# Opening set-up spread over ScalarE and VectorE, a second PSUM pool for one of the last sums, and a new table of priorities

## Chip, cores and metric

The kernel runs on 1 core of one Trainium2 chip. The metric is the device time of one execution in microseconds (us); the time before is the median of 3 runs, 860.9 us (860.76 to 861.0).

## The reference

Three stages follow one another: attention with a bucket mask, a gated feed-forward layer with an RMS norm, and a second feed-forward layer with an ELU.

```python
# q, k, v: (2, 8, 768, 64); proj: (64, 6)
q_bucket = sum over 6 bits of ((q @ proj) > 0) * 2**bit      # k_bucket likewise
scores = where(q_bucket[:, None] == k_bucket[None, :], q @ k.T / 8, -1e9)
attn = softmax(scores);  x = attn @ v         # x: (1536, 512), heads side by side
xn = x / sqrt(mean(x*x) + 1e-6) * rms_g
y  = (silu(xn @ w_gate) * (xn @ w_val)) @ w_out      # 512 -> 1536 -> 512
h  = y @ w_in                                        # 512 -> 2048
out = where(h > 0, h, exp(min(h, 0)) - 1) @ w_out2   # 2048 -> 512
```

## The kernel before

**Arithmetic.** TensorE works in fp32r; each fp32 operand is split into a rounded part (hi) and a remainder (lo), and products run in several passes.

**Attention.** The 16 heads are taken as 8 pairs (index j). The rows of a pair's q and k arrive in the tile raw by four DMAs (q and k of each of two heads a). twice (L326) copies each of the four into a tile rd, side by side with itself; prep_T (L337) transposes rd on TensorE in two halves (ps_t), ScalarE makes hi (L353), VectorE makes lo (L358), and GpSimd moves some rows across (L365, L368). prep_bits (L382) multiplies by the projection tile pj and VectorE writes the sign bits into one of two tiles bitt (L400). prep_count (L407) multiplies bitt by wsel to get the bucket match, which goes in as extra rows of the operands (L425, L427). Only then can score (L456) run: matmuls ps_s (L474), the row maximum nm on VectorE (L481), exp on ScalarE (L491), transposes of the weights ps_p (L519) with hi and lo (L527, L531), and the products with v (L566).

**The opening.** Before the first scores, ident and pj are made or cleared on GpSimd (setup, L1075), wsel is cleared there (L1100), and so are the two bitt tiles, with one row set to ones (setup_bits, L1102): a row that no bit is written to, so that the match carries a constant. VectorE writes a table of the numbers -1 and +1 for all bucket numbers (wtmp, setup_w), counts bits in ctmp (setup_count, L1089) and puts the parts of proj into pj (setup_pj, L1110). Small DMAs on the SP queue carry wtmp and ctmp into wsel. Dummy matmuls ps_w (L1143) keep TensorE at work from the moment ident exists.

**The feed-forward layers.** Weights arrive as 64-bit words, and ScalarE and VectorE turn them into fp32 (wf, L808 to L831), then into hi and lo (L852, L856). hidden makes ps_h (L905), reduce1 ps_y (L990), and reduce2 ps_o (L1044), which VectorE adds to the sums oa (L1056) before each block of 128 tokens is stored. ps_o uses the PSUM tag bank2 (2 buffers of two banks each); the tag bank has 4 buffers of one bank. The last block's columns are done in two cuts of 256.

**Order.** Nothing is issued as the code is written. Plan collects tasks with engine, assumed duration, reads and writes; Plan.order() lists them by earliest start and then by priority. The priorities of the attention tasks are a position (the unit number, 6 per pair, 48 in all) plus an entry of the table OFF; w0 and w0s in it place the first group of weights. Every engine then runs its own list in that order, so one changed assumption or entry can change the order of the whole attention stage.

```python
plan.add("DVE", 6.5, setup_count, [], [("h3", "ctmp")], -30)
plan.add("Pool", 3.1, setup_bits, [], ["bitt"], -29)
```

Of the kernel before, what the change touches and what calls it, by code (L numbers as in the profile page):

```python
# [12 lines left out]
AF = mybir.ActivationFunctionType  # L13
ALU = mybir.AluOpType
AX = mybir.AxisListType
# [7 lines left out]
PJP = -29.9  # L23
WARM = 16
POOL_COPY = 0.82
POOL_HALF = 0.57
POOL_CAST = 0.65
TURN = 0.13
BYPOOL = ([0, 1, 2, 3, 4], [0, 2, 3, 4], [0, 1, 2, 3, 4, 5], [2, 4], [2, 4], [2, 4], [2, 4], [0])
HOT = ('DVE', 'ACT', 'ACT', 'DVE')  # L30
BW = (384, 512)
OFF = {'S': [-0.384, -0.596, -1.82, 16.69, -0.785, -0.843, -0.281, -0.374], 'max': [107.091, 86.229, 74.287, 78.306, 4.65, 29.877, -1.002, 35.125], 'exp': [62.941, 112.551, 91.27, 19.546, 123.248, 62.234, 18.002, -5.545], 'T': [0.813, 0.913, 0.365, 0.876, 0.651, 1.113, 1.459, 0.993], 'hi': [19.733, -62.022, -7.959, -72.894, 51.659, 4.387, -74.284, -78.51], 'lo': [37.269, 76.285, 5.085, -95.768, -79.38, 8.342, -31.826, -0.586], 'V': [2.187, 1.975, 1.986, 1.909, 1.876, 2.208, 2.458, 2.096], 'my': [-17.276, -32.546, -64.73, -54.909, -121.029, -34.033, -7.347, -44.516], 'ld': [46.975, -7.846, 214.522, -35.192, 37.247, 221.876, -5.026, -66.279], 'pv': [56.573, -26.315, 46.952, -98.676, 75.721, 70.124, -94.292, -41.006], 'prep': [-0.879, -2.624, -3.589, -0.3, -0.223, -0.105, 0.276, -67.519], 'post': [5.051, 5.005, 2.459, 1.85, 3.722, 8.338, 2.173, 8.692], 'plo': [-134.549, 11.751, -83.073, -44.746, 0.084, -16.015, 72.021, -31.41], 'wc': -3.034, 'ld1': 96.489, 'norm0': -2.712, 'rush': 35.741, 'pstep': 0.316, 'qstep': 0.017, 'norm': 31.762, 'w0': 122.867, 'w0s': 1023313562453027.6}


class Plan:
# [143 lines left out]
def kernel(  # L179
# [14 lines left out]
    nc = tc.nc  # L194
    B, H, S, D = q.shape
    NB = proj.shape[1]
    NBK = 2 ** NB
# [4 lines left out]
    NC = S // 128  # L202
# [20 lines left out]
    def bank(name):  # L223
        return ps1.tile([128, 512], F32, tag="bank", name=name)

    def bank2(name):
        return ps2.tile([128, 2, 512], F32, tag="bank2", name=name)
# [11 lines left out]
    bitt = [const.tile([128, S], F32R, name=f"bitt{i}") for i in range(2)]  # L239
# [7 lines left out]
    plan = Plan(caps)  # L247

    def off(key, j):
        return OFF[key][j]  # L250

    def act(n, ptr=0):
        return n / 1200.0 + 0.05 + 0.093 * ptr

    def dve(n):
        return n / 960.0 + 0.069
# [10 lines left out]
    st = {}  # L267
# [57 lines left out]
        return (("slot", ("tq", "tk")[i], j, a), part)  # L325

    def twice(j, a, i, prio):
        def go():
            st["rd", j, a, i] = half([128, NC, 2, D], F32, "rd")
            nc.gpsimd.tensor_copy(  # L330
                out=st["rd", j, a, i], in_=st["raw", j][:, i, a].unsqueeze(2).to_broadcast([128, NC, 2, D])
            )

        plan.add("Pool", POOL_COPY, go, [(("slot", "raw", j), i, a)], [("h3", "rd", j, a, i)], prio)

    def prep_T(j, a, i, hf, prio):
        n = NC // 2  # L337
# [35 lines left out]
        if i == 0:  # L373
            plan.add("DVE", dve(HS), lo, [B_], top[:1], prio)
            plan.add("Pool", POOL_HALF, again, top[1:], [okey(j, a, i, ("dup", hf))], prio)
        else:
# [217 lines left out]
    def post(j, prio, step):  # L594
# [23 lines left out]

        plan.add("Pool", POOL_COPY, widen, [R_], [("h3", "rw", j)], prio)

# [137 lines left out]
    groups = []  # L758
# [17 lines left out]
    def weights(g, m, part, prio, gate):  # L776
# [19 lines left out]
        dma(load, 128 * cols * (8 if wide else 4), r=gate, w=[R_], prio=prio)  # L796
        prio += OFF["wc"]
        if wide:
# [232 lines left out]
    def reduce_cols(g, blk, t, tt, ds, prio):  # L1031
        li, f0, n, first, last = groups[g]
        wd = ds.stop - ds.start
        B_ = ("bank2", "o", g, tt, ds.start)
        A_ = ("slot", "oa", tt // 3)
        s = {}

        def pe(ft):
            if "ps" not in s:
                s["ps"] = bank2("ps_o")[:, 0, 0:wd]  # L1040
            wo = st["w", g]["wo"]
            h = st["h", g, blk, ft]
            for i, (wp, xp) in enumerate(PASS):
                nc.tensor.matmul(  # L1044
                    s["ps"], lhsT=h[:, xp, t * 128:(t + 1) * 128], rhs=wo[wp][:, ft, ds],
                    start=(ft == 0 and i == 0), stop=(ft == n - 1 and i == 2),
                )

        def copy():
            if ("oa", tt // 3) not in st:  # L1050
                st["oa", tt // 3] = slot([128, 3, DM], F32, "oa")
            nc.scalar.copy(out=st["oa", tt // 3][:, tt % 3], in_=s["ps"])

        def add():
# [14 lines left out]
        if first:
            plan.add("ACT", act(wd), copy, [B_], [(A_, tt % 3, 0)], prio)  # L1070
        else:
            plan.add("DVE", dve(wd), add, [B_], [(A_, tt % 3, ds.start)], prio)
        if last:
            dma(store, 128 * wd * 4, [(A_, tt % 3, ds.start)], [("out", tt, ds.start)], prio)
# [5 lines left out]
    def ones_of(t, i):  # L1080
        return t.rearrange("p (n t w) -> p n t w", t=2, w=2 ** i)[:, :, 1, :]
# [7 lines left out]
    def setup_count():  # L1089
        st["ctmp"] = half([1, 2, 2, NBK], F32, "ctmp")  # L1090
        c = st["ctmp"]
        nc.vector.memset(c[:, 1, 0], 0.0)
        for i in range(NB):
            t = ones_of(c[:, 1, 0], i)
            nc.vector.tensor_scalar(out=t, in0=t, scalar1=-1.0, scalar2=None, op0=ALU.add)
        nc.vector.tensor_copy(out=c[:, 1, 1], in_=c[:, 1, 0])
        nc.vector.tensor_scalar(out=c[:, 0], in0=c[:, 1], scalar1=1.0, scalar2=None, op0=ALU.add)

    def setup2():
        nc.gpsimd.memset(f(wsel), 0.0)  # L1100

    def setup_bits():  # L1102
        for t in bitt:
            nc.gpsimd.memset(f(t), 0.0)
            nc.gpsimd.memset(f(t[32:33]), 1.0)

    def setup3():
        nc.gpsimd.memset(ones, 1.0)
# [20 lines left out]
    plan.add("ACT", 0.02, lambda: nc.scalar.preload_act_table_set("natural_log_exp_and_others"), [], ["tab"], -40, tab="exp")  # L1129
    plan.add("Pool", 1.22, setup, [], ["ident", "pj0"], -30)  # L1130
    plan.add("DVE", 0.7, setup_w, [], [("h3", "wtmp")], -30)
    plan.add("DVE", 6.5, setup_count, [], [("h3", "ctmp")], -30)
    plan.add("Pool", 0.25, setup2, [], ["wsel0"], -29.5)
    plan.add("Pool", 3.1, setup_bits, [], ["bitt"], -29)
    plan.add("Pool", 0.2, setup3, [], ["ones"], -28)
    for a in range(2):
        dma(lambda a=a: ld_pj(a), 2000, [], [("pjf", a)], PJP)
# [24 lines left out]
    prep_v(0, -15)  # L1162
    load_qk(1, OFF["ld1"])

# [33 lines left out]
    for g in range(len(groups)):  # L1198
        li, f0, n, first, last = groups[g]
# [57 lines left out]
```

## Time and profile before

| what | value |
|---|---|
| median of 3 runs | 860.9 us |
| profiled execution, its own time | 861.95 us |
| its span, first to last instruction | 860.2 us |
| outside the span | 1.75 us |
| mean granted TensorE clock over the span | 0.995 |
| first scores on TensorE begin | 19.90 us |
| feed-forward work continuous on TensorE from | 302.56 us |
| last sum's matmuls begin | 855.60 us |

The span is what the rows below divide up. The profiled execution took 1.05 us longer than the median of the runs, 0.1%.

### The profile page before, as it was taken

To read this page: it belongs to the slowest core of one execution; us is meant where nothing else is said; L and a number is where in the kernel's file an instruction comes from. 1 tells how busy PE (TensorE), PEld (TensorE's weight loads), DVE (VectorE), ACT (ScalarE), POOL (GpSimd) and SP (SyncE) were. 2 spreads that over 40 slices of the span, in tenths; PEclk is the share of its full clock that TensorE was granted. 3 is DMA by queue.
4 is the path that set the end of the run, shared out by engine and by line. 5 is a ranking of instruction groups with operands and counts; after the bars stand their busy time and mean duration, and the time that the engine had idled before them with its cause. 6 is when DMAs were issued, how large, how long until landed. Compare 5 with 4: busy or idle time off the path is not lost.

```text
span 860.2 us, 12464 instructions
## 1 busy us (share of the span) xinstructions
PE 836.1 (97%) x4722; PEld 738.2 (86%) x4722; DVE 648.7 (75%) x1020; ACT 440.7 (51%) x831; POOL 279.2 (32%) x295
## 2 busy tenths in 40 slices
PE   7999999998999899999999999999999999999998
PEld 6899999887899799989889898887888888888786
DVE  8999899999999999443265555678856878677754
ACT  3889888898888655332222322245544333332321
POOL 8766576699745322110011110210201111111100
PEclk9999999999999999999999999999999999999999
DMA  5102012240002201211111312204221302001003
GB/s 165 39 19 64 12 38 75 60 146 35 19 2 75 74 1 38 85 31 44 49 50 50 98 50 99 74 1 146 74 74 37 110 25 74 25 25 50 1 12 135
DMA packets 25708, 49.05 MB, mean 57 GB/s; under 512 B 2480, under 2 KB 8880, under 8 KB 25648
## 3 DMA queue, kind: packets, MB, share of 16 engines
q1 hardware_dynamic: 25648, 48.25, 17.2%
q8 instruction: 37, 0.61, 0.3%
q14 instruction: 23, 0.19, 0.1%
HBM read 45.09 MB, written 3.15 MB: 56 GB/s over the span
## 4 chain that ended last, share of the span: by engine, by line
PE 80%; DVE 12%; ACT 4%; POOL 3%; issue 1%; POOLq 0%; DVEq 0%; ACTq 0%
PE ps_h L905 36%; PE ps_o L1044 14%; PE ps_y L990 11%; PE ps_s L474 5%; PE ps_v L566 5%; PE ps_p L519 5%; DVE pt L531 2%; PE ps_t L347 2%; DVE nm L481 2%; PE ps_b L395 1%; ACT p L491 1%; DVE wf L817 1%; DVE wf L824 1%; DVE wf L831 1%; ACT pt L527 1%
## 5 line engine op out<-in xcount | busy, mean ns | idle before, releaser
L856 POOL TENSOR_TENSOR wlo<-wf,whi 128x768 fp32r<-128x768 f32 (+1 forms) x54 | 87.4, 1618 | 444.8 <-ACT whi L852 430.5
L905 PE MATMUL ps_h<-xn,whi 128*128 128x512 f32 (+2 forms) x768 | 190.1, 336 | 2.9 <-DVE pt L531 1.1
L905 PEld LDWEIGHTS ps_h<-xn,whi 128*128 128x128 f32 x768 | 133.6, 189 | 15.6 <-DVE pt L531 1.4
L905 PE MATMUL ps_h<-xn,wlo 128*128 128x256 f32 (+2 forms) x384 | 128.9, 336 | 0.0
L1044 PE MATMUL ps_o<-whi,h 128*128 128x512 f32 (+1 forms) x388 | 118.9, 388 | 0.7 <-DVE oa L1056 0.6
L905 PE MATMUL ps_h<-y,whi 128*128 128x512 f32 x384 | 118.2, 389 | 0.0
L930 ACT ACTIVATE sg<-ps_h 128x512 f32<-128x512 f32 (+1 forms) x87 | 50.6, 583 | 112.6 <-PE ps_h L905 110.4
L852 ACT CAST whi<-wf 128x768 fp32r<-128x768 f32 (+1 forms) x54 | 39.6, 734 | 125.1 <-DVE wf L831 125.0
L566 PE MATMUL ps_v<-pt,vv 128*128 128x256 f32 x576 | 97.9, 296 | 2.2 <-DVE tk L358 1.0
L951 ACT CAST h<-hf 128x512 fp32r<-128x512 f32 (+1 forms) x87 | 51.7, 605 | 88.7 <-DVE hf L936 47.0
L481 DVE TENSOR_REDUCE nm<-ps_s 128x1 f32<-128x768 f32 x96 | 90.8, 946 | 3.1 <-PE ps_s L474 2.4
L990 PE MATMUL ps_y<-h,whi 128*128 128x512 f32 (+1 forms) x312 | 91.3, 373 | 1.3 <-DVE ya L1002 1.3
L491 ACT ACTIVATE p<-ps_s,nm 128x768 f32<-128x768 f32 x96 | 87.2, 909 | 8.3 <-DVE nm L481 7.6
L519 PE MATMUL ps_p<-ident,p 128*128 128x128 f32 x576 | 87.5, 278 | 3.4 <-DVE pt L531 2.6
L474 PE MATMUL ps_s<-tk,tq 128*128 128x384 f32 x384 | 88.2, 351 | 1.0 <-ACT p L491 0.9
L955 DVE TENSOR_TENSOR h<-hf,h 128x512 fp32r<-128x512 f32 (+1 forms) x87 | 69.5, 812 | 25.9 <-ACT h L951 25.1
L1044 PEld LDWEIGHTS ps_o<-whi,h 128*128 128x128 f32 x388 | 72.1, 188 | 16.7 <-DVE oa L1056 2.2
L905 PEld LDWEIGHTS ps_h<-y,whi 128*128 128x128 f32 x384 | 72.1, 188 | 15.0
L936 DVE TENSOR_TENSOR hf<-ps_h,sg 128x512 f32<-128x512 f32 (+1 forms) x39 | 25.2, 647 | 79.0 <-PE ps_h L905 79.0
L566 PEld LDWEIGHTS ps_v<-pt,vv 128*128 128x128 f32 x576 | 78.7, 189 | 5.4 <-DVE pt L531 1.9
L531 DVE TENSOR_TENSOR pt<-ps_p,pt 128x512 fp32r<-128x512 f32 x120 | 80.6, 681 | 3.6 <-ACT pt L527 2.2
L519 PEld LDWEIGHTS ps_p<-ident,p 128*128 128x128 f32 x576 | 67.3, 142 | 12.3 <-DVE pt L531 4.6
(109 smaller groups left out, 1521.3 us busy)
## 6 DMA issues: line engine op xcount, KB each, us to landing
wraw<-in_moe_w_out_dram SPq DMA_DIRECT2D x12, 768.0 KB, 5.1
wraw<-in_moe_w_in_dram SPq DMA_DIRECT2D x8, 768.0 KB, 4.7
wraw<-in_moe_w_out_dram SPq DMA_DIRECT2D x10, 512.0 KB, 4.0
raw<-in_q_dram SPq DMA_DIRECT2D x16, 192.0 KB, 3.1
raw<-in_k_dram SPq DMA_DIRECT2D x16, 192.0 KB, 3.5
vn<-in_v_dram SPq DMA_DIRECT2D x8, 384.0 KB, 3.2
wraw<-in_moe_w_gate_dram SPq DMA_DIRECT2D x4, 768.0 KB, 4.8
wraw<-in_moe_w_val_dram SPq DMA_DIRECT2D x4, 768.0 KB, 4.5
```

The costliest lines, as they stand in the source:

```text
L474: nc.tensor.matmul(st[B_][:, hf, 0:HS], lhsT=tq[:, x, c * 128:(c + 1) * 128], rhs=tk[:, x, hf * HS:(hf + 1) * HS], start=(x == 0), stop=(x ...
L481: nc.vector.tensor_reduce(out=st["nm", u, cc], in_=st[B_][:, :, 0:HS], axis=AX.XY, op=ALU.max, negate=True,)
L491: nc.scalar.activation(out=halves(st["p", u][:, cc]), in_=st.pop(B_)[:, :, 0:HS], func=AF.Exp, bias=st["nm", u, cc], scale=1.0, accum_out= ...
L519: nc.tensor.transpose(out=st[B_][:, o:o + 128], in_=p[:, cc, (2 * n + kt) * 128:(2 * n + kt + 1) * 128], identity=ident,)
L531: nc.vector.tensor_tensor(out=pt[:, 1], in0=st.pop(B_), in1=f(pt[:, 0]), op=ALU.subtract)
L566: nc.tensor.matmul(st[B_][:, 0:256], lhsT=st["vv", j][:, a, 2 * n + kt, :], rhs=pt[:, x, kt * 256:(kt + 1) * 256], start=(n == seq[0] and ...
L856: nc.gpsimd.tensor_tensor(out=l, in0=s["w"], in1=f(h), op=ALU.subtract)
L905: nc.tensor.matmul(ps[:, o:o + ln], lhsT=w[wp][:, kk, ft * 128:(ft + 1) * 128], rhs=t[xp][:, s:s + ln], start=(kk == 0 and n == 0), stop=( ...
L951: nc.scalar.copy(out=st["h", g, blk, ft][:, 0, 0:bw], in_=s["hf"])
L955: nc.vector.tensor_tensor(out=h[:, 1, 0:bw], in0=s["hf"], in1=f(h[:, 0, 0:bw]), op=ALU.subtract)
L990: nc.tensor.matmul(s["ps"][:, 0:bw], lhsT=wo[wp][:, ft, m * 128:(m + 1) * 128], rhs=h[:, xp, 0:bw], start=(ft == 0 and i == 0), stop=(ft = ...
L1044: nc.tensor.matmul(s["ps"], lhsT=h[:, xp, t * 128:(t + 1) * 128], rhs=wo[wp][:, ft, ds], start=(ft == 0 and i == 0), stop=(ft == n - 1 and ...
```

## The change

Five edits. setup_bits moves from GpSimd to ScalarE and is done by four Copy activations of ident with scale 0 (bias 1 for the row of ones), so it now waits for ident. setup_count takes three VectorE operations and reads wtmp. The first pair's four copies in twice go to GpSimd, VectorE, GpSimd and ScalarE, in the order q, k of the first head, then q, k of the second. In the last group, for the last two blocks of 128 tokens, every second sum takes its PSUM from the tag bank. All entries of OFF are new.

```diff
+FIRST = ('Pool', 'DVE', 'Pool', 'ACT')
-OFF = {'S': [-0.384, -0.596, -1.82, 16.69, ...], ..., 'w0': 122.867, 'w0s': 1023313562453027.6}
+OFF = {'S': [-0.746, -0.843, -1.864, 66.85, ...], ..., 'w0': 189.461, 'w0s': 3.7229545865993564e+29}
...
     def twice(j, a, i, prio):
+        eng = FIRST[2 * a + i] if j == 0 else "Pool"
...
-            nc.gpsimd.tensor_copy(
-                out=st["rd", j, a, i], in_=st["raw", j][:, i, a].unsqueeze(2).to_broadcast([128, NC, 2, D])
-            )
-        plan.add("Pool", POOL_COPY, go, [(("slot", "raw", j), i, a)], [("h3", "rd", j, a, i)], prio)
+            cp = {"Pool": nc.gpsimd.tensor_copy, "DVE": nc.vector.tensor_copy, "ACT": nc.scalar.copy}[eng]
+            cp(out=st["rd", j, a, i], in_=st["raw", j][:, i, a].unsqueeze(2).to_broadcast([128, NC, 2, D]))
+        us = {"Pool": POOL_COPY, "DVE": dve(S), "ACT": act(S) + 0.04}[eng]
+        plan.add(eng, us, go, [(("slot", "raw", j), i, a)], [("h3", "rd", j, a, i)], prio)
...
-        B_ = ("bank2", "o", g, tt, ds.start)
+        spare = groups[g][4] and tt >= B * S // 128 - 2 and (tt + ds.start // wd) % 2
+        B_ = ("bank" if spare else "bank2", "o", g, tt, ds.start)
...
-                s["ps"] = bank2("ps_o")[:, 0, 0:wd]
+                s["ps"] = bank("ps_o")[:, 0:wd] if spare else bank2("ps_o")[:, 0, 0:wd]
...
-        nc.vector.memset(c[:, 1, 0], 0.0)
-        for i in range(NB):
-            t = ones_of(c[:, 1, 0], i)
-            nc.vector.tensor_scalar(out=t, in0=t, scalar1=-1.0, scalar2=None, op0=ALU.add)
-        nc.vector.tensor_copy(out=c[:, 1, 1], in_=c[:, 1, 0])
-        nc.vector.tensor_scalar(out=c[:, 0], in0=c[:, 1], scalar1=1.0, scalar2=None, op0=ALU.add)
+        nc.vector.tensor_reduce(
+            out=c[:, 1, 0], in_=st["wtmp"].rearrange("o i n -> o n i"), axis=AX.X, op=ALU.add
+        )
+        nc.vector.tensor_scalar(
+            out=c[:, 0], in0=c[:, 1, 0].unsqueeze(1).to_broadcast([1, 2, NBK]), scalar1=-0.5,
+            scalar2=1.0 - 0.5 * NB, op0=ALU.mult, op1=ALU.add,
+        )
+        nc.vector.tensor_scalar(
+            out=c[:, 1], in0=c[:, 0], scalar1=-1.0, scalar2=None, op0=ALU.add
+        )
...
     def setup_bits():
+        wide = ident.unsqueeze(1).to_broadcast([128, NC, 128])
         for t in bitt:
-            nc.gpsimd.memset(f(t), 0.0)
-            nc.gpsimd.memset(f(t[32:33]), 1.0)
+            v = t.rearrange("p (c n) -> p c n", n=128)
+            nc.scalar.activation(out=v, in_=wide, func=AF.Copy, scale=0.0)
+            nc.scalar.activation(out=v[32:33], in_=wide[32:33], func=AF.Copy, bias=1.0, scale=0.0)
...
-    plan.add("DVE", 6.5, setup_count, [], [("h3", "ctmp")], -30)
+    plan.add("DVE", 2.2, setup_count, [("h3", "wtmp")], [("h3", "ctmp")], -30)
-    plan.add("Pool", 3.1, setup_bits, [], ["bitt"], -29)
+    plan.add("ACT", 2.9, setup_bits, ["ident"], ["bitt"], -29)
```

## Rows read from the trace of the kernel before

**Rows 1.** Windows: length, then busy time per engine, TensorE clock, DMA share, GB/s.

```profile
0.00:20.00 20.00, 14.80 (x82) 13.05 (x83) 15.99 (x37) 7.70 (x15) 17.18 (x33) 0.91 0.58 178
...
12.00:13.00 1.00, 1.00 (x7) 0.92 (x5) 1.00 (x3) 0.91 (x3) 0.72 (x3) 0.50 0.75 226
...
20.00:302.56 282.56, 269.30 (x1921) 250.11 (x1919) 268.50 (x427) 239.91 (x498) 187.06 (x215) 0.99 0.16 50
302.56:856.60 554.04, 552.04 (x2722) 475.03 (x2722) 363.81 (x557) 193.13 (x318) 74.93 (x48) 1.00 0.17 56
...
280.00:300.00 20.00, 16.79 (x112) 15.73 (x111) 19.77 (x30) 12.08 (x21) 6.74 (x4) 1.00 0.24 79
```

**Rows 2.** Chain that ended last, in order of time: start, length, what.

```profile
5.55 2.32 POOL rd L330 x3
7.87 0.79 DVE pj L1114
...
299.93 2.12 DVE wf L811
```

**Rows 3.** Timeline of the opening: start, length, engine, line, operation, idle before.

```profile
0.73 1.28 ACT L1129 ACT_TABLE_LOAD   x1 [0.73 <-PEq L1241]
0.73 0.40 SPq L275 DMA_DIRECT2D raw<-in_q_dram  x1
1.65 0.43 SPq L275 DMA_DIRECT2D raw<-in_q_dram  x1
...
2.17 0.74 POOL L1104 MEMSET bitt<- 128x768 f32 x1
2.60 1.21 SPq L1123 DMA_DIRECT2D pj_f<-in_proj_dram  x2
...
6.95 0.87 ACT L353 ACTIVATE tq<-ps_t 128x384 fp32r<-128x384 f32 x2 [4.94 <-PE ps_t L347]
...
10.57 2.68 PE L347 MATMUL ps_t<-ident,rd 128*128 128x128 f32 x15 [1.77 <-DVE tq L358]
...
13.17 1.20 DVE L358 SCALAR_TENSOR_TENSOR tk<-ps_t,tk 128x384 fp32r<-128x384 f32 x2
...
19.90 0.94 PE L474 MATMUL ps_s<-tk,tq 128*128 128x384 f32 x4
```

**Rows 4.** Timeline of ACT and DVE, 283 to 303 us.

```profile
283.49 1.28 ACT L930 ACT_TABLE_LOAD   x1
284.78 0.49 ACT L930 ACTIVATE sg<-ps_h 128x384 f32<-128x384 f32 x1
...
298.16 0.83 ACT L852 CAST whi<-wf 128x768 fp32r<-128x768 f32 x1 [1.48 <-DVE wf L831]
298.90 0.92 ACT L808 ACTIVATE wf<-wraw 128x768 f32<-128x768 f32 x1
...
302.54 0.56 DVE L817 TENSOR_SCALAR wf<-wf 128x768 int32<-128x768 int32 x1
```

**Rows 5.** DVE's groups from 0 to 22 us: busy, mean ns, idle before.

```profile
L1095 DVE TENSOR_SCALAR ctmp<-ctmp 1x32 f32<-1x32 f32 x6 | 4.5, 744 | 0.2
...
L358 DVE SCALAR_TENSOR_TENSOR tk<-ps_t,tk 128x384 fp32r<-128x384 f32 x5 | 2.8, 551 | 0.3 <-ACT tk L353 0.2
```

**Rows 6.** DMAs of the opening: time from issue to landing, raw's first.

```profile
DMA to landing us min/median/max: 2.7/4.3/5.4
...
raw<-in_q_dram SPq DMA_DIRECT2D x1, 192.0 KB, 3.7
...
pj_f<-in_proj_dram SPq DMA_DIRECT2D x2, 1.5 KB, 3.3
```

**Rows 7.** Timeline of the end.

```profile
854.85 1.13 DVE L1056 TENSOR_TENSOR oa<-ps_o,oa 128x512 f32<-128x512 f32 x2 [0.67 <-PE ps_o L1044]
...
855.24 0.28 PE L1044 MATMUL ps_o<-wlo,h 128*128 128x256 f32 x1
855.60 0.51 PE L1044 MATMUL ps_o<-whi,h 128*128 128x256 f32 x2
```

More of the change, by code (lines that the diff above doesn't have):

```diff
@@ L31 @@
 BW = (384, 512)
-OFF = {'S': [-0.384, -0.596, -1.82, 16.69, -0.785, -0.843, -0.281, -0.374], 'max': [107.091, 86.229, 74.287, 78.306, 4.65, 29.877, -1.002, 35.125], 'exp': [62.941, 112.551, 91.27, 19.546, 123.248, 62.234, 18.002, -5.545], 'T': [0.813, 0.913, 0.365, 0.876, 0.651, 1.113, 1.459, 0.993], 'hi': [19.733, -62.022, -7.959, -72.894, 51.659, 4.387, -74.284, -78.51], 'lo': [37.269, 76.285, 5.085, -95.768, -79.38, 8.342, -31.826, -0.586], 'V': [2.187, 1.975, 1.986, 1.909, 1.876, 2.208, 2.458, 2.096], 'my': [-17.276, -32.546, -64.73, -54.909, -121.029, -34.033, -7.347, -44.516], 'ld': [46.975, -7.846, 214.522, -35.192, 37.247, 221.876, -5.026, -66.279], 'pv': [56.573, -26.315, 46.952, -98.676, 75.721, 70.124, -94.292, -41.006], 'prep': [-0.879, -2.624, -3.589, -0.3, -0.223, -0.105, 0.276, -67.519], 'post': [5.051, 5.005, 2.459, 1.85, 3.722, 8.338, 2.173, 8.692], 'plo': [-134.549, 11.751, -83.073, -44.746, 0.084, -16.015, 72.021, -31.41], 'wc': -3.034, 'ld1': 96.489, 'norm0': -2.712, 'rush': 35.741, 'pstep': 0.316, 'qstep': 0.017, 'norm': 31.762, 'w0': 122.867, 'w0s': 1023313562453027.6}
+OFF = {'S': [-0.746, -0.843, -1.864, 66.85, -0.744, -0.758, -0.224, -0.41], 'max': [86.06, 128.957, 190.513, 53.124, 102.143, -5.035, -10.834, 24.749], 'exp': [119.567, 67.059, 76.291, 2.774, 75.069, 56.662, -35.846, 43.868], 'T': [0.573, 0.48, 0.307, 0.831, 0.703, 1.127, 1.259, 1.321], 'hi': [36.303, -33.663, 1.961, -57.136, 22.322, 57.959, -91.469, -121.974], 'lo': [-34.121, 9.653, 32.465, -109.77, -12.636, -87.223, -67.192, -11.818], 'V': [2.027, 1.953, 1.894, 2.015, 1.865, 2.222, 2.417, -11.303], 'my': [76.979, -114.216, -55.16, -8.134, -134.423, -45.978, -63.486, -29.752], 'ld': [16.116, 103.645, 134.666, -130.684, 51.199, 277.906, -45.786, 44.455], 'pv': [19.903, -68.605, 49.828, -156.296, 63.827, 116.499, -168.838, 19.653], 'prep': [-0.809, -2.78, -3.346, -0.341, -0.21, -0.194, 0.226, -82.459], 'post': [4.851, 4.774, 2.643, 1.592, 3.332, 9.244, 3.712, 28.29], 'plo': [-227.264, -10.728, 0.013, -54.307, -64.379, -36.39, 74.399, -48.961], 'wc': 0.693, 'ld1': 50.459, 'norm0': -125.474, 'rush': 27.318, 'pstep': 0.316, 'qstep': 0.146, 'norm': -8.853, 'w0': 189.461, 'w0s': 3.7229545865993564e+29}
 class Plan:
```

## Prediction

> **What bounds the kernel now.** I read the windows by stage first, then the chain, then the timeline at the two ends. The windows show three stages. From 302.56 to 856.6 us TensorE is busy 552.0 of 554.0 us: the feed-forward stage is TensorE's own work at the full clock, and nothing in the change alters that work. From 20 to 302.56 us TensorE is idle for 13.3 us of 282.6 and VectorE for 14.1; both are nearly full and wait for each other by turns. In the first 20 us TensorE is idle for 5.2 us, the mean granted clock is 0.91, and from 12 to 13 us it is 0.50, the lower of its two levels (1.2 against 2.4 GHz), behind a hole of 1.77 us before the matmuls at 10.57 us [rows 1, 3]. So time can be won at the opening, in the attention stage's holes, and in the last microseconds. The chain names what sets the opening: GpSimd's copies rd to 7.87 us, which begin only at 5.5 us, and then VectorE's pj [rows 2]. The first scores start at 19.90 us [rows 3].
>
> **The bit tiles.** Four GpSimd memsets begin at 2.17 us and take 0.74 us each [rows 3], with gaps 3.1 us; they leave GpSimd, and the copies behind them no longer wait. On ScalarE, which stands idle from 2.01 to 6.95 us [rows 3], there come four Copy operations of 768 elements a row. The nearest row is the 128x768 cast, 0.83 us, whose successor starts 0.74 us after it did [rows 4]; four take 4 x 0.74 + 0.1 = 3.1 us, from 2.01 to 5.1 us. That idle time hides them. If the cover is too short, the first hi waits: with its transposes ready at about 4.8 us (below) that is 0.3 us. At 0.92 us each, the length of the other 768-element operation there [rows 4], and no overlap, they end at 5.7 us and cost 0.9 us. Bounds 0 and 0.9 us lost; I take 0.3, since the cast is the nearer row.
>
> The table load stands ahead of them. In the trace the activation behind a load of 1.28 us starts 0.01 us after its end [rows 4], so I let them start at 2.01 us. The Trainium skill, "ScalarE: Activation LUTs", section "What ACT_TABLE_LOAD costs", counts a drain of about 1.38 us on top of the 1.28 us; by that the four would end at 6.5 us. The trace does not show such a drain behind the load. It is a rival below.
>
> **The count table.** Removed from VectorE: a memset, six 32-element operations at 744 ns [rows 5], a copy and one more. At the same rate the eight take 6.0 us, and pj stands behind them at 7.87 us [rows 2]. Added: three operations of at most 384 elements. They cost between nearly nothing and 0.77 us each, somewhat over the rate at which the old ones went beside GpSimd's memsets; GpSimd still clears pj and wsel until 2.17 us [rows 3], so I take 0.4 us each, 1.2 us together. Even the full 2.3 us would end near 4 us, before VectorE has anything else: no row has landed. The SP queue gains too: the small DMA from ctmp no longer holds up the second pair's rows.
>
> **The copies.** The first q row is issued at 0.73 us [rows 3] and the shortest landing of a row is 2.7 us [rows 6]: 3.4 us. The second q row is issued at 1.65 us and lands 3.7 us later, at 5.35 us [rows 3, 6]; rows are issued about 0.46 us apart, so I put the last k row at 5.9 us. GpSimd's three copies on the chain take 2.32 us, 0.77 us each [rows 2]. It copies q of head 0 from 3.4 to 4.2 us, where it began at 5.5 us, then waits for the second q row, 5.35 to 6.1 us. VectorE copies k of head 0 from about 4.0 us; a 768-element operation with one source takes 0.56 us at best [rows 4] and, held by GpSimd's copy beside it, twice that, so it ends by 5.2 us. ScalarE copies the last k row after 5.9 us in 0.74 us, between two hi's. The first transposes are done at about 4.8 us and the first hi moves from 6.95 us [rows 3] to about 5.1 us. The price of the copies on the two new engines is 0.6 to 1.1 us and 0.74 us; both engines stood idle or at the ctmp operations then.
>
> **What is late next.** Not the rows any more but VectorE. proj lands at 2.60 + 0.6 + 3.3, the second half's issue included, about 6.2 us [rows 3, 6]. setup_pj takes about 2.2 us (from 7.87 us to the lo that TensorE waits for at 10.57 us, less that lo's 0.5 us) [rows 2, 3], and its priority puts it ahead of the lo's: 6.2 to 8.4 us. One lo fits before it; seven remain at 0.55 us [rows 5], 8.4 + 3.9 = 12.3 us. Before, the eight ended at 14.4 us [rows 3]. That is 2.1 us. From there to the first scores lay 5.5 us, in which the bit matmuls began at half the clock [rows 1]. If TensorE is fed without the hole at 10.57 us, six bit matmuls of a half take about 1 us instead of 2, and 1.2 us more comes off. I therefore put the shift at 3.3 us. Its lower bound is 2.0 us, at the old clock. Its upper bound is VectorE's net work, 6.1 us out and 1.2 and 0.8 us in: 4.1 us. GpSimd comes free some 4 us earlier as well (3.1 us of memsets, two copies of 0.8 us), so the v tiles and the second pair's copies follow.
>
> **The tail.** Of the three sums of the last two blocks only the first cut of the last block moves to the tag bank. Before, the last cut began at 855.60 us, when the block ahead gave up its bank2 buffer; the cut in between issued its last matmul at 855.24 us [rows 7], so with another buffer the next follows about 0.09 us behind, at 855.33 us. That is 0.27 us, all of it at the end, since the last add and store hang on these matmuls. VectorE's adds last until 855.98 us [rows 7], before the last cut's matmuls end, so they do not take the gain away. ps_h is finished by then, so a bank is free. Bounds 0 and 0.27 us.
>
> **The new priorities.** They set the order of all attention tasks and of the first weights, but remove no work. From these rows their effect has no sign; I take 0, and bound it by the holes: TensorE's idle time from 20 to 302.56 us is 13.3 us [rows 1], a quarter of it 3.3 us, to be won or lost.
>
> **Sum.** 3.3 us at the opening and 0.27 us at the end make 3.6 us. Off the span of 860.2 us that leaves 856.6 us, off the profiled execution's 861.95 us 858.4 us. That execution lay 1.05 us above the median, so the median comes to 857.3 us. A measurement of this kernel can tell about 0.2%, 1.7 us, from no change.
>
> **Rivals.**
>
> First, the forecast: the opening is 2 to 4.1 us shorter and attention is carried along whole, 855 to 859 us. For it: after 20 us TensorE and VectorE are both 95% busy [rows 1], so an earlier start can be lost only in new holes. Chance 0.48.
>
> Second, the shift is absorbed. The seam to the feed-forward stage is set by weight conversions on VectorE, of which a step of 2.12 us stands last on the chain before 302.56 us [rows 2]; if these are no earlier, the seam is not. Against it: they too are VectorE work, and VectorE has 4 us less of it. 859.2 to 862.6 us, chance 0.18.
>
> Third, slower: with w0 raised, the weight conversions bunch at the seam. From 280 to 300 us VectorE is busy 19.77 of 20 us and TensorE idle 3.2 us [rows 1]. Three more steps of 2.12 us in TensorE's way cost 6.4 us: 857.3 + 6.4 = 863.7 us. It decides from the point where TensorE's idle time from 20 to 303 us grows by 5.3 us, the 3.6 us won and the 1.7 us that can be told. Chance 0.16.
>
> Fourth, the new order also closes a quarter of the holes: 854.0 us. Chance 0.13.
>
> Fifth, ScalarE is not ready at 2.01 us but 1.4 us later, because a table load blocks it longer than its row. The first hi then starts at 6.5 us, only 0.45 us earlier than before. Eight hi's at 0.44 us [rows 3] and a copy of 0.74 us end at 10.8 us, ahead of VectorE's last lo, so half of the 1.4 us is lost: 858.0 us. Against it is the activation at 284.78 us [rows 4]. Chance 0.05.
>
> **How the numbers follow.** Faster by over 0.2%: the first, fourth and fifth, 0.66. Within 0.2%: 0.17, nearly all of the second. Slower: 0.17, the third and the end of the second. As cases of both signs hold weight, the range runs from 853.0 us, which takes in the fourth with the opening's upper bound, to 862.6 us, the end of the second; the third's price lies outside it. The forecast's own range is 855 to 859 us.
>
> **What the changed profile would show.** Right: four operations of ScalarE on bitt between 2.0 and 5.2 us; three on ctmp that end before 4 us; rd on three engines, the first hi near 5.1 us; pj from 6.2 us; first scores between 15.8 and 17.9 us; continuous ps_h from about 299.3 us; some 554 us from there to the last matmuls; no wait for oa before the last cut. Wrong: a first hi after 6 us, a copy held up by the engine beside it for more than its own length, or first scores 3 us earlier and ps_h no earlier than 302 us. The forecast fails most easily by the order: if TensorE's idle time from the first scores to the seam differs from 13.3 us by more than 3.3 us.

## The result, and the profile after

The kernel after takes 852.49 us (852.03 to 853.11), against 860.88 us before. The ratio is 0.9903 with an interval of 0.9886 to 0.992: 8.4 us faster, more than twice the 3.6 us of the forecast and just below the range. In the profiled executions the span went from 860.2 to 851.1 us, 9.1 us. That is more than the 8.4 us of the medians, because the profiled execution of the kernel before took 1.05 us more than its median. Its trace shows TensorE at the lower of its two clock levels twice: at 12 to 13 us [rows 1], and once more behind 220 us, as in this window (same columns):

```profile
221.00:222.00 1.00, 1.00 (x7) 1.00 (x6) 0.86 (x2) 0.66 (x3) 0.62 (x1) 0.50 0.00 0
```

Windows of the kernel after, at the cuts of [rows 1]; same columns:

```profile
0.00:20.00 20.00, 17.16 (x101) 15.52 (x102) 13.52 (x37) 13.34 (x25) 14.17 (x29) 1.00 0.56 178
...
12.00:13.00 1.00, 0.44 (x3) 0.39 (x3) 0.26 (x1) 0.00 (x0) 0.94 (x2) 1.00 0.95 304
...
280.00:300.00 20.00, 18.06 (x114) 17.04 (x113) 19.84 (x29) 11.29 (x19) 7.03 (x4) 1.00 0.10 41
```

In the first 20 us TensorE starts 101 matmuls instead of 82, VectorE is busy 2.5 us less, ScalarE 5.6 us more and GpSimd 3.0 us less. These cuts mix stages that moved, so I cut both traces at four events instead: the first scores, the last scores, the first ps_y and the end. I call the third stretch the seam: the last pair's weights, the norm and the first hidden blocks. Windows of the kernel before:

```profile
0.00:19.90 19.90, 14.70 (x82) 12.95 (x82) 15.89 (x37) 7.70 (x15) 17.08 (x33) 0.91 0.58 179
19.90:279.80 259.90, 250.93 (x1803) 233.16 (x1802) 246.13 (x395) 226.41 (x476) 178.79 (x211) 0.99 0.15 48
279.80:318.50 38.70, 34.41 (x209) 32.46 (x208) 37.81 (x55) 22.81 (x37) 12.29 (x6) 1.00 0.13 41
318.50:860.20 541.70, 536.10 (x2636) 459.62 (x2634) 348.88 (x536) 183.82 (x304) 71.01 (x46) 1.00 0.18 58
```

And of the kernel after:

```profile
0.00:15.20 15.20, 12.80 (x72) 11.78 (x73) 8.85 (x29) 9.62 (x16) 9.44 (x23) 1.00 0.56 171
15.20:275.70 260.50, 251.96 (x1826) 235.40 (x1826) 249.09 (x403) 228.45 (x483) 181.13 (x215) 1.00 0.16 52
275.70:309.40 33.70, 31.70 (x193) 29.89 (x192) 31.30 (x48) 22.26 (x36) 10.72 (x6) 1.00 0.14 47
309.40:851.10 541.70, 535.94 (x2636) 459.60 (x2634) 349.22 (x537) 184.56 (x306) 71.97 (x46) 1.00 0.18 58
```

The 9.1 us are 4.7 before the first scores, 0.6 lost in the scores stretch and 5.0 won at the seam. From the first ps_y to the end both take 541.7 us.

The scores stretch and the seam have to be read together, since work crossed the cut between them: in the kernel after 12 matmuls ps_h of the first hidden blocks run before the last scores, in the kernel before none. So of the seam's 5.0 us 2.7 are work that TensorE no longer does there (busy 34.41 and 31.70 us), and 2.3 are idle time (4.3 and 2.0 us). Both stretches together are 4.4 us shorter. TensorE's idle time in them, length less busy time, falls from 13.3 to 10.5 us; of the rest about 1 us is the lower clock behind 220 us. That is an estimate from e1 below, which has the old order, a clock of 1.00 and 297.6 us for the two, where the kernel before has 298.6.

The opening of the kernel after, timeline as in [rows 3]:

```profile
0.73 1.28 ACT L1139 ACT_TABLE_LOAD   x1 [0.73 <-PEq L1251]
1.63 0.81 DVE L1096 TENSOR_REDUCE ctmp<-wtmp 1x64 f32<-1x384 f32 x1
2.02 0.84 ACT L1114 ACTIVATE bitt<-ident 128x768 fp32r<-128x768 f32 x1
2.48 0.21 DVE L1099 TENSOR_SCALAR ctmp<-ctmp 1x128 f32<-1x128 f32 x1
2.73 0.21 DVE L1103 TENSOR_SCALAR ctmp<-ctmp 1x128 f32<-1x128 f32 x1
...
3.22 0.82 POOL L334 COPY rd<-raw 128x768 f32<-128x768 f32 x1 [0.84 <-DMA raw<-in_q_dram]
3.65 0.81 DVE L334 COPY rd<-raw 128x768 f32<-128x768 f32 x1 [0.70 <-DMA raw<-in_k_dram]
...
4.63 0.84 ACT L1115 ACTIVATE bitt<-ident 1x768 fp32r<-1x768 f32 x1
5.28 0.83 POOL L334 COPY rd<-raw 128x768 f32<-128x768 f32 x1 [1.24 <-DMA raw<-in_q_dram]
5.80 0.83 ACT L334 COPY rd<-raw 128x768 f32<-128x768 f32 x1 [0.32 <-DMA raw<-in_k_dram]
6.24 0.17 DVE L1124 CAST pj<-pj_f 128x6 fp32r<-128x6 f32 x1 [1.79 <-POOL rd L334]
6.54 0.86 ACT L356 ACTIVATE tq<-ps_t 128x384 fp32r<-128x384 f32 x2
...
9.85 0.56 DVE L361 SCALAR_TENSOR_TENSOR tk<-ps_t,tk 128x384 fp32r<-128x384 f32 x1 [1.23 <-ACT tk L356]
...
11.25 1.01 DVE L361 SCALAR_TENSOR_TENSOR tk<-ps_t,tk 128x384 fp32r<-128x384 f32 x2
```

The changed operations stand where the prediction put them: bitt directly behind the table load, ctmp done at 2.94 us, each copy behind its own row's landing, the last lo's end at 12.26 us. The first hi does not: it starts at 6.54 us, not near 5.1. TensorE in the kernel after, on to the first scores:

```profile
13.95 0.51 PE L419 MATMUL ps_c<-bitt,wsel 128*128 128x384 f32 x2
14.75 0.61 PE L419 MATMUL ps_c<-bitt,wsel 128*128 128x384 f32 x2 [0.29 <-DVE bitt L403]
15.20 0.75 PE L477 MATMUL ps_s<-tk,tq 128*128 128x384 f32 x3
...
16.79 0.88 PE L350 MATMUL ps_t<-ident,rd 128*128 128x128 f32 x6
```

The same stretch of the kernel before:

```profile
16.15 0.51 PE L416 MATMUL ps_c<-bitt,wsel 128*128 128x384 f32 x2
17.30 0.55 PE L347 MATMUL ps_t<-ident,rd 128*128 128x128 f32 x3 [0.64 <-POOL rd L330]
17.61 0.59 PE L416 MATMUL ps_c<-bitt,wsel 128*128 128x384 f32 x2
18.24 0.55 PE L347 MATMUL ps_t<-ident,rd 128*128 128x128 f32 x3
19.62 0.52 PE L347 MATMUL ps_t<-ident,rd 128*128 128x128 f32 x3 [0.84 <-DVE tq L427]
```

From the first match matmul (ps_c) to the first scores it is 3.75 us before ([rows 3] have the 19.90) and 1.25 us after. Before, three groups of the second pair's transposes stand in TensorE's queue ahead of the first scores and wait there, once for a GpSimd copy and once for VectorE; after, they stand behind them. That is the order, not an operation of the diff.

At the seam, TensorE's waits from 276 to 320 us, before:

```profile
PE ps_x L624 <- DVE pt L531: 1.3, 1, 1.3
PE ps_h L905 <- DVE pt L531: 1.1, 1, 1.1
PE ps_h L905 <- DVE ot L584: 1.1, 1, 1.1
PE ps_h L905 <- DVE hf L936: 0.7, 1, 0.7
```

and after:

```profile
PE ps_v L569 <- DVE pt L534: 1.2, 1, 1.2
PE ps_h L908 <- DVE hf L939: 0.7, 1, 0.7
```

Two of four waits are gone, 4.2 us of waiting have become 1.9. The first ps_h now starts at 271.6 us, before the last scores (275.7); before it was 281.8, behind them (279.8).

The end of the kernel after:

```profile
840.53 0.40 PE L1048 MATMUL ps_o<-whi,h 128*128 128x256 f32 x2
...
846.70 0.40 PE L1048 MATMUL ps_o<-whi,h 128*128 128x256 f32 x2
...
847.29 0.28 PE L1048 MATMUL ps_o<-wlo,h 128*128 128x256 f32 x1
```

The last cut (from 846.70 us) waits for nothing; the gap of [rows 7] is gone. The other cut of 256 columns now runs 6 us ahead of it, at 840.53 us.

### The profile page after: what moved, and what is told of

It reads as the page before. It is cut to its first block, busy times and chain, and to the rows that moved or that the text cites. A ratio compares the mean times of both kernels' runs of the same rounds, so it can differ in the third digit from the quotient of the medians.

```text
span 851.1 us, 12464 instructions
## 1 busy us (share of the span) xinstructions
PE 832.4 (98%) x4722; PEld 736.7 (87%) x4722; DVE 638.5 (75%) x1015; ACT 444.9 (52%) x838; POOL 273.3 (32%) x289
## 4 chain that ended last, share of the span: by engine, by line
PE 81%; DVE 13%; ACT 4%; issue 1%; POOL 1%; ACTq 0%; DVEq 0%; POOLq 0%
PE ps_h L908 37%; PE ps_o L1048 14%; PE ps_y L993 11%; PE ps_p L522 5%; PE ps_v L569 5%; PE ps_s L477 4%; DVE nm L484 3%; DVE pt L534 3%; PE ps_t L350 2%; PE ps_b L398 2%; ACT p L494 1%; ACT pt L530 1%; DVE wf L827 1%; DVE wf L834 1%; PE ps_w L1153 1%
## 5 line engine op out<-in xcount | busy, mean ns | idle before, releaser
L908 PEld LDWEIGHTS ps_h<-xn,wlo 128*128 128x128 f32 x384 | 72.6, 189 | 5.5
```

Of the source, the lines that this page charges most:

```text
L908: nc.tensor.matmul(ps[:, o:o + ln], lhsT=w[wp][:, kk, ft * 128:(ft + 1) * 128], rhs=t[xp][:, s:s + ln], start=(kk == 0 and n == 0), stop=( ...
```

## The experiments

All runs at a glance. Times of TensorE's events and the span in us, from each run's profile; ratio to the kernel before on the same chip, with interval. "Ops" are the three edits of the opening's operations, "costs" the durations and engines that the planner assumes for them, "table" is OFF.

| run | first ps_s | last ps_s | first ps_y | span | ratio |
|---|---|---|---|---|---|
| before | 19.9 | 279.8 | 318.5 | 860.2 | 1 |
| after | 15.2 | 275.7 | 309.4 | 851.1 | 0.9903 |
| e1 new ops, old order | 18.7 | 277.6 | 316.3 | 857.6 | 0.9985 [0.9976, 0.9995] |
| e2 old ops, new order | 17.0 | 277.7 | 311.4 | 853.5 | 0.9924 [0.991, 0.9939] |
| e3 after, old table | 15.1 | 276.3 | 315.0 | 856.4 | 0.9961 [0.9946, 0.9976] |
| e4 before, new table | 19.8 | 281.2 | 315.0 | 857.2 | 0.9968 [0.9956, 0.998] |
| e17 before, new costs | 17.1 | 278.4 | 317.2 | 858.6 | 0.9994 [0.9984, 1.0003] |
| e9 bits on GpSimd | 15.9 | 276.5 | 310.3 | 853.5 | 0.9925 [0.9909, 0.9942] |
| e10 old count | 14.6 | 275.4 | 309.2 | 850.8 | 0.9898 [0.9883, 0.9912] |
| e11 copies on GpSimd | 15.2 | 275.8 | 309.5 | 852.4 | 0.9911 [0.9896, 0.9926] |
| e12 no spare bank | 14.3 | 274.9 | 308.6 | 850.6 | one run |
| e5 after, old V entry | 15.1 | 271.9 | 313.3 | 855.0 | 0.9942 [0.9927, 0.9957] |
| e6 before, new V entry | 19.5 | 283.1 | 329.8 | 871.3 | 1.0151 [1.0136, 1.0166] |
| e7 after, old last pair | 14.3 | 273.2 | 317.4 | 859.0 | 0.9992 [0.9982, 1.0001] |
| e8 before, new last pair | 19.5 | 280.7 | 319.4 | 861.8 | 1.0038 [1.0024, 1.0052] |
| e15 after, old weight entries | 14.3 | 274.8 | 308.4 | 849.8 | 0.9887 [0.9872, 0.9902] |
| e16 = e8 with new weight entries | 19.9 | 282.0 | 320.7 | 863.3 | 1.006 [1.0043, 1.0076] |
| e18 after, old early pairs | 14.2 | 277.7 | 316.6 | 858.6 | 1.0002 [0.9992, 1.0011] |
| e13 before, no GpSimd lo | 19.8 | 280.3 | 317.0 | 858.9 | 0.9999 [0.9989, 1.0008] |
| e14 after, no GpSimd lo | 14.2 | 274.2 | 306.5 | 848.2 | 0.9866 [0.9851, 0.9881] |

The first scores of kernels with the same opening scatter from 14.2 to 15.2 us, so a difference under 1 us in that column says nothing.

**Operations or order: e1, e2.** e1 keeps every engine's list as before and emits the new operations in it; e2 keeps the new lists and emits the old operations on their old engines.

```diff
# e1: before.py; plan.add lines (costs, priorities) and OFF untouched
-    setup_count, setup_bits, twice as before
+    setup_count, setup_bits, twice as in the change
# e2: after.py; plan.add lines and OFF untouched
-    setup_count, setup_bits, twice as in the change
+    setup_count, setup_bits, twice as before
```

> The issue order of the kernel before, kept whole, with the changed opening's operations in it (bit tiles on ScalarE, three count operations, copies on three engines); no spare bank. Theory A (the opening's 4.7 us carry through attention, the new order adds the other 3.7 us): 856 to 857 us, first scores near 15.5 us. Theory B (the opening is all of it): 852.5 us. Theory C (the order is all of it): 860 to 861 us even though the first scores come earlier.

> The issue order of the changed kernel, kept whole, with the old opening's operations in it (memsets and all four copies on GpSimd, nine count operations on VectorE); spare bank kept. A: 852.5 + 4.7 = 857 us. B: 860.5 us. C: 852.5 to 853.5 us.

The operations alone bring 0.15%, 1.3 us; the order alone 0.76%, 6.5 us. Together that is 7.8 of the 8.4 us: nearly additive. Of these theories C came nearest (e1's 860.48 us lies in its range, e2's 855.40 between A and C), and B fell. The operations bring the first ps_c from 16.15 to 14.71 us, and the old order then gives most of it back. TensorE in e1:

```profile
14.71 0.52 PE L417 MATMUL ps_c<-bitt,wsel 128*128 128x384 f32 x2
16.16 0.55 PE L348 MATMUL ps_t<-ident,rd 128*128 128x128 f32 x3 [0.93 <-POOL rd L333]
...
18.48 0.52 PE L348 MATMUL ps_t<-ident,rd 128*128 128x128 f32 x3 [1.09 <-DVE tq L428]
18.75 0.94 PE L475 MATMUL ps_s<-tk,tq 128*128 128x384 f32 x4
```

The same transposes stand ahead of the scores, and the two waits have grown by 0.3 us each: 4.04 us from ps_c to ps_s.

**Table or assumed costs: e3, e4, e17.** The order comes from both.

```diff
# e3: after.py               # e4: before.py
-OFF = {new}                 -OFF = {old}
+OFF = {old}                 +OFF = {new}
# e17: after.py, new plan.add lines kept
-OFF = {new}; setup_count, setup_bits, twice as in the change
+OFF = {old}; setup_count, setup_bits, twice as before
```

> The changed kernel with the old table of priorities; the planner orders it anew with the new assumed costs. A: 855 to 857 us. B: 852.5 us. C: 859 us or more. Any of them may be off by the luck of a fresh order; that is what this run sizes: if it lies more than 2 us from the run with the old order and the new operations, a fresh order alone moves the time by that much.

> The kernel before with the new table of priorities alone. A: 857 us if the table is good by itself; B: 861 us; C: 853 us. If the table is only good together with the costs that it was made for, this is not better than 861 us, whatever the other three give.

> The old table and the old opening operations, but the changed kernel's assumed costs and engines in the planner: only the order of the opening follows. Theory Z (the assumed cost of the count, 2.2 for 6.5 us, takes the second pair's transposes from ahead of the first scores): first scores at 17.0 us as in the run with the new order and the old operations, 38.7 us at the seam, 858 to 860 us. Otherwise (the new table does it): 19.5 us and 861 us.

The two places divide cleanly. The first scores come early (15.1, 17.1 us) where the assumed costs are new, whatever the table, and stay at 19.8 us in e4, where only the table is. The seam is short (33.8 us) in e4 and long (38.7, 38.8) in e3 and e17: it goes by the table. e3's 858.57 us lies between theories A and C; in e4 the table by itself gains 2.7 us. TensorE in e17, with the old operations and the old table:

```profile
15.81 0.51 PE L419 MATMUL ps_c<-bitt,wsel 128*128 128x384 f32 x2
16.62 0.62 PE L419 MATMUL ps_c<-bitt,wsel 128*128 128x384 f32 x2 [0.29 <-DVE bitt L403]
17.07 0.75 PE L477 MATMUL ps_s<-tk,tq 128*128 128x384 f32 x3
```

The first ps_c is hardly earlier than before (15.81), but the transposes are out of the way: 1.26 us to the scores. So the 4.7 us of the opening are 2.8 us of order and the rest operations, each give or take the scatter above.

By itself that earlier start is worth nothing measurable at the end. e17's first scores and seam came as theory Z said, its time did not: 861.09 us and not 858 to 860, a gain of 0.5 us, inside its interval. Its scores stretch is 261.3 us, 1.4 longer. TensorE's idle time from the first scores to the first ps_y, computed as above, is 13.8 us in e17 and 13.7 in e3, both with the old table; it is 11.7 in e4 and 10.5 in e2. With the old operations, then, the costs alone bring 0.5 us, the table alone 2.7, and both together (e2) 6.5: the two are worth more together than apart.

**The parts of the opening under the new order: e9, e10, e11, e12.**

```diff
# e9: after.py, setup_bits
-    nc.scalar.activation(out=v, in_=wide, func=AF.Copy, scale=0.0); ...
+    nc.gpsimd.memset(f(t), 0.0); nc.gpsimd.memset(f(t[32:33]), 1.0)
# e10: after.py, setup_count as before
# e11: after.py, twice
-    cp = {"Pool": nc.gpsimd.tensor_copy, ...}[eng]
+    cp = nc.gpsimd.tensor_copy
# e12: after.py, reduce_cols
-    s["ps"] = bank("ps_o")[:, 0:wd] if spare else bank2("ps_o")[:, 0, 0:wd]
+    s["ps"] = bank2("ps_o")[:, 0, 0:wd]
```

> The changed kernel's issue order, kept whole, with the bit tiles cleared by GpSimd's memsets again; the three count operations and the copies on three engines stay. Of the 1.8 us by which the old operations made the first scores later under this order (17.0 for 15.2 us). Theory G (GpSimd's memsets are the cost, by what stands behind them and by holding VectorE's small operations): first scores 16 to 17 us, count operations 0.7 us each. Theory H (VectorE's nine count operations are the cost): 15.2 to 15.6 us.

> The changed kernel's issue order with the nine old count operations; bit tiles on ScalarE and the copies stay. G: the old operations are short once no memset runs beside them, about 0.2 us each instead of 0.74 after 2.4 us, the count ends near 4 us, first scores 15.2 to 15.5 us. H: it ends near 8 us again, pj and the lo's wait for it, first scores near 17 us.

> The changed kernel's issue order with all four first copies on GpSimd; bit tiles on ScalarE and the short count stay. If spreading the copies is worth something: first scores 16 us or later. If the rows' landing sets them and not the engine: within 0.3 us of 15.2, or earlier, since ScalarE's first hi no longer stands behind its copy.

> The changed kernel's issue order with all last sums in bank2. The wait of 0.28 us ahead of the last cut's matmuls is back if the spare bank removed it; the end from the first ps_y on is longer by 0.25 to 0.3 us. If not, nothing changes.

Of the three edits of operations only the memsets put the first scores outside the scatter: back on GpSimd they make them 0.7 us later than in the kernel after, 1.7 later than in the earliest of its equals. GpSimd then copies the first q row at 5.79 us, behind the memsets, where the kernel after does it at 3.22 us, and the first hi starts 0.70 us later, at 7.24 us. The intervals of the times overlap, so at the end this is not shown. The old count costs nothing. The copies on GpSimd cost nothing outside the scatter: in e11 the first hi starts 0.8 us earlier, at 5.74 us, but VectorE's pj, beside the copies, takes 2.1 us and not 1.0.

With the spare bank removed the last cut still does not wait, but the bank is worth something at another place. In e12 the two cuts of 256 columns begin at

```profile
839.74 0.47 PE L1048 MATMUL ps_o<-whi,h 128*128 128x256 f32 x2
...
846.23 0.40 PE L1048 MATMUL ps_o<-whi,h 128*128 128x256 f32 x2
```

6.49 us apart, against 6.17 in the kernel after, and the stretch from the first ps_y to the end is 542.0 us for 541.7. The expected 0.25 to 0.3 us came, in the one execution that there is.

Of the 2.4 and 1.3 us by which e9's and e11's spans are longer than after's, 1.2 us each is the last store, which landed 3.1 us after its issue and not 1.9.

e10 and e9 also show why the old count was slow. VectorE in e10, the old count with the bitt memsets gone from GpSimd (a row for all six operations):

```profile
1.71 1.72 DVE L1099 TENSOR_SCALAR ctmp<-ctmp 1x32 f32<-1x32 f32 x6
```

and in e9, new count beside the memsets:

```profile
2.48 0.51 DVE L1099 TENSOR_SCALAR ctmp<-ctmp 1x128 f32<-1x128 f32 x1
3.02 0.76 DVE L1103 TENSOR_SCALAR ctmp<-ctmp 1x128 f32<-1x128 f32 x1
```

The six took 744 ns each beside memsets of 0.74 us [rows 3, 5]; here, without them, their mean is 258 ns. The new ones take 0.21 us in the kernel after and up to 0.76 in e9. H fell. G held in what it says of the operations, which are not slow in themselves but last longer beside GpSimd's memsets; its first scores came at 15.9 us, just under its 16. The Trainium skill, "GPSIMD Engine Reference", section "1. Specifications", says that GpSimd shares its SBUF interfaces with VectorE and that VectorE operations of certain modes contend with it. The traces fit that, and add the size: an operation of 32 elements lasted 744 ns, as long as the whole memset of 0.74 us beside it.

**Why is the seam shorter? e5 to e8, e15, e16, e18.** Entries of the table were exchanged: V of the last pair, which ranks that pair's products with v against the first hidden blocks; all of the last pair's entries with rush and norm; the weights' entries; all but the last pair's.

```diff
# e5: after.py                          # e6: before.py
-'V': [..., -11.303]                    -'V': [..., 2.096]
+'V': [..., 2.096]                      +'V': [..., -11.303]
# e7: after.py / e8: before.py: entry 7 of every list, 'rush', 'norm'
-'S': [..., -0.41], 'max': [..., 24.749], ..., 'rush': 27.318, 'norm': -8.853
+'S': [..., -0.374], 'max': [..., 35.125], ..., 'rush': 35.741, 'norm': 31.762   (e8: the reverse)
# e15: after.py / e16: e8 with the reverse
-'wc': 0.693, 'w0': 189.461, 'w0s': 3.7229545865993564e+29
+'wc': -3.034, 'w0': 122.867, 'w0s': 1023313562453027.6
# e18: after.py with OFF as before, but entry 7 of every list, 'rush', 'norm' as in the change
```

> The changed kernel with one entry of the table put back: V of the last pair (2.096 for -11.303), which ranks that pair's products with v against the first hidden layer. Theory D (this entry sets the seam: the time from the last scores to the last products with v was 18.3 us under every order with the old table and 13.9 under every order with the new): 18 us there and 856.5 to 857.5 us. Theory E (the seam is set by other entries of the last pair together, or by the first weights): 13.9 us and 852 to 853.5 us.

> The kernel before with only that entry new. D: 14 us from the last scores to the last products with v, 3 to 5 us faster than before. E: 18 us, within 1 us of before.

> The changed kernel with all entries of the last pair, and rush and norm, put back. D and the wider form of E (some entry of the last pair does it): 18 us, 856.5 to 857.5 us. A third, F (the seam follows from the earlier entries and w0, which shift what VectorE has left of the weight conversions by then): 14 us and 852 to 854 us.

> The kernel before with all new entries of the last pair, and rush and norm. D and E: 14 us, 3 to 5 us faster than before. F: 18 us, within 1 us of before.

> The changed kernel with the three entries of the table that rank the weights' loads and conversions (w0, w0s, wc) put back; the planner orders anew. Theory X (the seam is short because these entries bring conversions forward, 17 of 32 before the last scores for 12): 12 to 14 conversions by then, 37 to 39 us from the last scores to the first ps_y, 856 to 858 us. Theory Y (they do nothing by themselves): 17 and 33.7 us, 852 to 853.5 us.

> The kernel before with the new entries of the last pair, rush, norm, and the three of the weights. X: 33.7 us from the last scores to the first ps_y, about 857 us. Y: 38 us or more, 860 us or more. If Y holds here and X in the other run, no part of the table is good outside the whole.

> The changed kernel with the last pair's new entries, rush and norm, and everything else of the table old. With all old the seam (last scores to first ps_y) took 38.7 us, with all new 33.7, with only the last pair old 44.2. If the last pair's entries make the seam by themselves under the new assumed costs: 33.7 us and about 853 us. If it needs the whole table: 38 us or more, 857 us or more.

The V entry is not the cause (theory D): alone in the old table it makes the seam 46.7 us, with TensorE idle for 9.8 of them and a mean clock of 0.85, and the kernel 13 us slower. Nor are all the last pair's entries (e8 38.7 us, e18 38.9), nor these with the weights' (e16 38.7). In the other direction the weights' entries are indifferent (e15 33.6), while the last pair's are needed (e7 44.2). None of the times forecast for e5 to e8 came: e6, e7 and e8 were slower than any theory allowed.

Every mixture in which attention entries of the two tables meet has a seam of 38.7 to 46.7 us. Part of that goes with the clock: in all six mixtures TensorE is at the lower level for a part of the seam, with a mean of 0.85 in e6, 0.92 in e7 and 0.96 in the others, where the kernels with one whole table have 1.00. The seam of e18, columns as above:

```profile
277.70:316.60 38.90, 36.09 (x217) 35.02 (x216) 37.18 (x60) 23.60 (x40) 9.50 (x6) 0.96 0.14 42
```

TensorE's idle time in it is 2.8 us, nearer the 2.0 of the kernel after than the 4.3 of the kernel before, but it is busy for 36.1 us instead of 34.4, and the scores stretch has more idle time (12.2 us against 9.0). So the last pair's entries do shorten the waits at the seam, and lose it elsewhere. With the whole old table the seam is 38.7 to 38.8 us, with the whole new one, whether or not the weights' entries are old, 33.6 to 33.8. That the new order leaves fewer conversions of weights for the seam (theory W: 16 of some 32 against 20) fell too: e8 and e16 had 16 left, e6 13, and no gain.

**Collisions with GpSimd: e13, e14.** Before, a conversion at the seam is sometimes twice its usual length, as here beside a GpSimd wlo of 2.56 us. VectorE and GpSimd in the kernel before:

```profile
296.00 2.13 DVE L831 SCALAR_TENSOR_TENSOR wf<-wraw,wf 128x768 int32<-128x768 int32 x1
...
294.75 2.56 POOL L856 TENSOR_TENSOR wlo<-wf,whi 128x768 fp32r<-128x768 f32 x1 [4.75 <-ACT whi L852]
```

In e13 and e14 the first group's wlo becomes a copy on ScalarE; the low part of these weights is then not computed.

```diff
# both, in lo()
-            nc.gpsimd.tensor_tensor(out=l, in0=s["w"], in1=f(h), op=ALU.subtract)
+            if g == 0:
+                nc.scalar.copy(out=l, in_=s["w"])
+            else:
+                nc.gpsimd.tensor_tensor(out=l, in0=s["w"], in1=f(h), op=ALU.subtract)
```

> The kernel before, its issue order kept whole; the low part of the first group's weights is not computed: ScalarE writes a copy of the weights in its place, where GpSimd subtracted (so the output is not the reference's). Those eight subtractions of 1.85 us and more run beside VectorE's conversions. Under every order with the old table VectorE's sixteen single-source conversions before the first ps_y took 15.5 us, under every order with the new table 10.9 us. Theory S (GpSimd's subtractions hold VectorE's conversions, and the new order has fewer of them side by side): the sixteen fall to 9 to 11 us, the first ps_y comes at 313 to 315 us for 318.5. Theory W (the seam is set by how many conversions are left behind the last scores, 20 under the old table, 16 under the new): the first ps_y stays within 1.5 us of 318.5.

> The changed kernel's issue order with the same replacement (the low part of the first group's weights is not computed). S: little left to gain, the sixteen fall from 10.9 to 9 or 10 us, the first ps_y comes 0 to 2 us earlier than 309.4. W: as in the other run, within 1.5 us. If both runs gain the same 4 us or more, the collisions are no part of what tells the two orders apart.

The same conversion in e13:

```profile
295.63 0.94 DVE L831 SCALAR_TENSOR_TENSOR wf<-wraw,wf 128x768 int32<-128x768 int32 x1
```

Without these GpSimd operations the seam falls by 2.0 us in the old order and by 1.4 us in the new one. VectorE's sixteen single-source conversions up to the first ps_y, which theory S put at 9 to 11 us in e13, still take 14.5 (15.4 before), so these subtractions are not all that lengthens them. The difference between the orders stays, 36.7 against 32.3 us, so theory S falls as the reason for it. At the end the old order gained nothing measurable from it (0.9999), the new one 0.4% (0.9866 against 0.9903).

No version that computes the whole result clearly beats the kernel after: e15 (0.9887) and e10 (0.9898) lie inside its interval.

## Why the prediction missed

**The step that failed** is "The new priorities": "From these rows their effect has no sign; I take 0, and bound it by the holes", a quarter of 13.3 us. With the old operations the order alone is worth 6.5 us (e2), twice that bound, and the operations, which the forecast took for everything, 1.3 us (e1). Two things were wrong in the step. The order took 2.8 us of TensorE's idle time after the first scores (13.3 to 10.5 us; e1 to after the same, 13.4 to 10.5), near the end of the bound instead of its middle. And the bound counted only idle time behind 20 us, though the order also decides what stands ahead of the first scores: 2.8 us more, by e17. The row was there to be read: the transposes between ps_c and ps_s in TensorE's queue.

**The opening.** Forecast 3.3 us with bounds 2.0 and 4.1; measured 4.7. Up to the last lo it is the forecast's 2.1 us (14.37 and 12.26), but by luck: pj took 1.2 us less than forecast, and VectorE then waited 1.23 us for ScalarE before the lo at 9.85 us. Behind the last lo 1.2 us should come off by the clock of the bit matmuls; 2.6 came off, of which 2.5 lie between the first ps_c and the first scores, where the transposes stood. The clock term was wrong: from 12 to 13 us the clock was 0.50 in the profile before [rows 1], but e4 and e13 ran the old opening at 1.00, with the same hole ahead of it (1.76 and 1.77 us), and began the scores at 19.8 us, 0.1 earlier. Their bit matmuls were done sooner, and the waits behind them were longer, 0.94 and 1.09 us in e4 for the 0.64 and 0.84 shown above. The operations alone bring 1.2 us (e1) to 1.8 us (e2 to after), under the lower bound.

**Bit tiles.** 0.84 us each, 3.45 us together (forecast 3.1): they did not overlap. The first hi began at 6.54 us and not 5.1, which the prediction had named as a sign of being wrong, since ScalarE's copy of the last k row, 5.80 to 6.63 us, stood ahead of it. The fifth rival fell: the first bitt starts 0.01 us after the load's end. The Trainium skill, "ScalarE: Activation LUTs", section "What ACT_TABLE_LOAD costs", counts a drain of about 1.38 us on top of the load; behind this load the trace does not show it.

**Count, copies, pj.** The count took 1.23 us (forecast 1.2). pj took 1.0 us from 6.24 us, not 2.2: no GpSimd copy ran beside it, as one did in e11 (2.1 us). None of this set the end (e10, e11).

**The tail.** Forecast 0.27 us; from before to after 0.0, since both stretches behind the first ps_y are 541.7 us. The gap of [rows 7] is gone without the spare bank too (e12), because the other cut of 256 columns runs earlier. It does so in e3 and e17 as well, but not in e1 and e4, so this comes with the plan's edits and not with the table. In the new order the bank is worth 0.3 us at another place (e12, one execution): the size was right, the place was not. What takes the 0.3 us away between before and after was not isolated.

**Rivals.** The second, the shift absorbed, did not come in the kernel after, but it is what e17 shows: 2.8 us at the first scores, 0.5 at the end. The third, bunched conversions, did not come: VectorE is as full from 280 to 300 us (19.84 us), but TensorE's idle time there fell from 3.2 to 1.9 us. The fourth, the order closing a quarter of the holes, 854.0 us at a chance of 0.13, was the nearest, in time and in what it says of the idle time (2.8 us for 3.3). The prediction said that it fails most easily by the order, if that idle time moved by more than 3.3 us; it failed by the order with 2.8.

**What stays open.** Why the new table makes the seam 5 us shorter, beyond the work that it moves ahead of the last scores. Shown: neither the V entry nor the last pair's entries bring it without the others, the weights' entries play no part, and neither the number of conversions left nor the wlo collisions explain it alone. In the traces the first ps_h precedes the last scores (in every run with the short seam, and in e6) and two of four waits are missing; which of the many moves in the lists brings that about was not isolated.

## What to carry to other kernels

Where a planner builds every engine's list from assumed costs, an edit of costs or priorities is a change of its own: ask first what stands in the bounding engine's queue ahead of the first critical instruction, and time old operations in the new order and new operations in the old one. Do not price a reorder at zero; give it a term as wide as the idle time it can touch, the opening's included. An entry taken out of a tuned table can be worth the opposite of what it brings in the whole.

## What was unexpected on the hardware

- VectorE operations on one partition and 32 elements lasted as long as the GpSimd memset beside them (744 ns, against 258 ns in e10).
- A last store of the same size landed 1.9 us after its issue in some kernels (after, e10) and 3.1 us in others (e9, e11); no run shows why.
- A hole of the same length ahead of the same matmuls went with the lower clock level in one profile (before, 1.77 us) and with the full one in others (e4 and e13, 1.76 and 1.77 us), and the lower level there moved the first scores by 0.1 us.
- Only the order of the same attention work moved the seam from 33.6 to 46.7 us; in the longest (e6), with TensorE idle for 9.8 us, the mean granted clock was 0.85 too.
